# Expert tiles of 816 rows instead of 832, with the last partial tile transposed first

## The chip, the cores and the metric

The kernel runs on one core of a Trainium2 chip. The core has five engines with an instruction stream each: TensorE (PE in the profile; PEld is its weight load), VectorE (DVE), ScalarE (ACT), GpSimd (POOL) and SyncE (SP), which here only issues transfers. The metric is the device time of one execution, from the first to the last instruction with what lies around them, in microseconds (us). The median over several runs is compared.

## The reference

```python
# attention: delta rule, state (48 x 48) per batch and head, 768 steps
for t in range(S):
    y[:, :, t] = q[:, :, t] @ state
    v_old = state.T @ k_n[:, :, t]
    state = state + beta[t] * outer(k_n[:, :, t], v[:, :, t] - v_old)
x = y.transpose(0, 2, 1, 3).reshape(3072, 384)
# router: top 2 of 8 experts for each token
noisy = x @ w_gate + log1p(exp(x @ w_noise)) * noise
top2, top2_w = two largest of noisy, their softmax
# experts
for e in range(8):
    for k in range(2):
        mask = top2[:, k] == e
        h = maximum(x[mask] @ w1[e], 0)          # 384 -> 1024
        out[mask] += top2_w[mask, k] * (h @ w2[e])   # 1024 -> 384
```

All values are float32. There are 3072 tokens with two experts each, so an expert has 768 tokens on average. Evaluated with its own seed, the reference sends 711, 771, 789, 774, 756, 744, 807 and 792 tokens to the experts 0 to 7.

## The kernel before, in words

**Two stages.** `deltanet` (L470) computes attention and the router up to about 390 us; its order comes from a planner (`Jobs`, with costs and due times). While it runs, tokens are entered in a list for each expert (`tokens_x` in HBM: token number, gate, place of its row in `rows_y`), and the first five tiles of expert 0 are computed. The change touches nothing that the planner orders.

**How an expert is laid out.** Each expert takes a fixed number of rows, `ROWS = TILES * 128 + MORE`: six full tiles of 128 tokens and one partial tile of `MORE` tokens. An index past the list is out of bounds and is skipped by the transfers. `count` is the largest number of tokens of any expert; if it is over `ROWS`, a last branch (L1855) computes the remaining tiles of all experts one by one.

**What one expert does.** The loop `for e in range(1, E)` (L1775) is a written-out order, and every engine runs its own instructions in that order. For each expert:

- `first` (L1632) multiplies by `w1` as a fast block product: 20 products of blocks (`FACTORS`), each for two 128-column pieces, in place of 24. One operand is a block of `w1` or a sum of blocks (`s_w`), the other is half of the expert's rows (`RH = ROWS // 2` columns of `xe`, or a sum `s_x`). `PLAN` is the list of products, copies, additions and ReLUs, with the PSUM bank (`inner`) of each. The float32 products are two PE instructions each in the trace, so an expert has 80 of them (L1591, tile `inner`), then ACT copies (L1658) or DVE adds (L1652) the result to `hT`.
- `sums_of_hidden` (DVE, L1579) forms sums of the hidden blocks, and `second` (L1660) multiplies by `w2` in blocks of 192 columns (L1591, 192 columns moved), with the gate applied by DVE (L1487, L1491). It treats six full tiles as three pairs (tile i of the first three with tile i of the last three). The three are `pairs[0]`, `pairs[1]` and `pairs[2]`.
- `last_rows` (L1694) does the partial tile: its `MORE` tokens are the stationary operand, and two results are built side by side, one in partitions from 0, one in partitions from 64 (`halves`); DVE adds both (L1706).
- `put` (L1782) issues POOL's indirect transfer that adds a tile to the output (L460).

**The next expert's rows.** During expert e, POOL gathers the rows of expert e+1 into `xr` (`load_rows`, L405), SP rearranges them to `xq` with 16 transfers (`regroup`, L1605), and DVE turns 32 x 32 blocks (`turns`, L1615) into `xe`. The turns are a generator of seven instructions: six for full tiles (three chunks k of the first three tiles, then three of the last three) and one for the partial tile. They are placed two at a time behind the steps n = 5, 6, 3, 7, 4 of `second` for `pairs[0:2]` (L1826). After the turns that follow n = 7, DVE runs five additions of `SUMS_X` on the new `xe` (L1832), then the gates of n = 4; the first of them reads the bank `outer[0]`, which step n = 1 of `pairs[2]` overwrites (L1837).

The columns of `hT` and `xe` are laid out as first three tiles, partial tile, last three tiles: `full = [0:MAIN], [MAIN+MORE:ROWS]` with `MAIN = 384`, while `half` cuts at `RH`.

**Expert 0's remainder** is `rest` (L1709): tile 5 and the partial tile, `cols = 128 + MORE` columns, 48 PE instructions at L1742, then L1752 for tile 5 and L1757 for the partial tile, which is built side by side as in `last_rows`.

Of the kernel before, what the change touches and what calls it, by code (L numbers as in the profile page):

```python
# [21 lines left out]
Q = 32  # L22
QS = 128 // Q
TILES = 6
MORE = 64
EARLY_BANK = 2, (0, 1, 2)
EARLY = {2: [(0, 2)], 4: [(2, 4), (4, 5)]}
EARLY_TILES = 5
# [4 lines left out]
PUT_IN_RULE = -1  # L33
ROWS = TILES * 128 + MORE
META = 3
# [202 lines left out]
def kernel(  # L238
# [51 lines left out]
    KT = DM // 128  # L290
    FT = F // 128
    NT = N // 128
# [110 lines left out]
    def take_rows(got, index, units):  # L403

        d = nc.gpsimd.indirect_dma_start(  # L405
            out=got, out_offset=None, in_=rows_y[0 : units * 128],
            in_offset=bass.IndirectOffsetOnAxis(ap=index, axis=0),
            bounds_check=units * 128 - 1, oob_is_err=False,
        ).ins
        tc.add_to_no_dep_group("taken", d)  # L410
        for n, i in stored:
            if n < units:
                tc.add_manual_dep(d, i.name, SYNC, reason="rows stored before they are read")
        return d

    metas_x = const.tile([128, E, TILES + 1, META], FP32, name="metas_x")
    early_x = [const.tile([128, DM], FP32, name=f"early_x{i}") for i in range(EARLY_TILES)]
    early_meta = const.tile([128, EARLY_TILES, META], FP32, name="early_meta")
    rest_x = const.tile([128, TILES + 1 - EARLY_TILES, DM], FP32, name="rest_x")
    rows_in = [128] * TILES + [MORE]  # L420

# [15 lines left out]
    def place_of(meta):  # L437
        return meta[..., 2:3].bitcast(I32)
# [1060 lines left out]
    with ExitStack() as ectx:  # L1499
# [18 lines left out]
        FT2, MAIN = FT // 2, TILES // 2 * 128  # L1518
# [5 lines left out]
        xr = moe.tile([128, TILES + 1, DM], FP32, name="xr")  # L1524
        xq = moe.tile([128, QS, TILES + 1, DM // QS], FP32, name="xq")
        xe = moe.tile([128, KT, ROWS], FP32, name="xe")
# [11 lines left out]
        half = [slice(0, RH), slice(RH, ROWS)]  # L1538
        full = [slice(0, MAIN), slice(MAIN + MORE, ROWS)]

# [54 lines left out]

        def load_rows(e):
            for i, size in enumerate(rows_in):
                take_rows(xr[0:size, i], place_of(metas_x[0:size, e, i]), NT)

        def regroup(queues=(nc.sync,)):  # L1600

            for g in range(QS):
                tiles = TILES + (g * Q < MORE)
                for c in range(QS):
# [7 lines left out]
        def turns():  # L1612

            def turn(out, in_):
                return lambda: nc.vector.transpose(out=out, in_=in_)  # L1615

            some = TILES // 2
            for i in range(2):
                for k in range(KT):
                    yield turn(  # L1620
                        xe[:, k, full[i]].rearrange("p (i g x) -> p i g x", i=some, g=QS),
                        xq[:, :, i * some : (i + 1) * some, k : DM // QS : KT].rearrange(
                            "p g i j -> p i g j"
                        ),
                    )
            more = MORE // Q
            yield turn(
                xe[:, :, MAIN : MAIN + MORE].rearrange("p k (g x) -> p k g x", g=more),
                xq[:, 0:more, TILES].rearrange("p g (j k) -> p k g j", k=KT),
            )  # L1630

        def first(a1, sums):  # L1632

# [75 lines left out]
        def rest():  # L1709
# [6 lines left out]
            load_metas(1)  # L1716
            load_metas(0)
            load_rows(1)
            for i, size in enumerate(rows_in[t0:]):
                take_rows(rest_x[0:size, i], place_of(metas_x[0:size, 0, t0 + i]), NT)  # L1720
# [26 lines left out]
            for turn in turns():  # L1747
                turn()
# [26 lines left out]
        for e in range(1, E):  # L1775
# [36 lines left out]
            if follows:  # L1812
                load_rows(e + 1)
                regroup()
                add_up(nc.gpsimd, SUMS_W, blocks[0])
# [5 lines left out]
            for emit in of_hidden[1][2:4]:  # L1821
                emit()
            both(2, 1)
            turning = turns() if follows else iter(())
            sums_x = SUMS_X if follows else []
            for n in (5, 6, 3, 7, 4):  # L1826
# [28 lines left out]
    with tc.If(count > ROWS):  # L1855
        for e in range(E):
            with tc.tile_pool(name=f"left{e}", bufs=1) as pool:
                w1e, w2e = load_weights(weight_tiles(pool), e)
                earlier, added = added, []
                for i in range(TILES, NT):  # L1860
# [8 lines left out]
                    xr = pool.tile([128, DM], FP32, name="xrl")  # L1869
                    take_rows(xr, place_of(meta), NT)  # L1870
                    got = pool.tile([128, DM], FP32, name="gotl")
                    xe = pool.tile([128, KT, 128], FP32, name="xel")
# [53 lines left out]
```

## Time and profile before

| | |
|---|---|
| median of 4 runs | 834.45 us (827.36 to 837.58) |
| profiled execution | 833.76 us |
| its span, first to last instruction | 831.9 us |
| mean granted TensorE clock | 0.868 over the span, 1.00 in the experts |
| PE busy, whole span | 736.6 us (89%) |
| DVE, POOL, ACT busy | 542.2, 419.0, 308.6 us |
| one expert of the loop, start to start | 58.5 us |

The experts 1 to 7 run from 409.05 to 818.2 us; in front of them is `rest` from 391 us, behind them some 13.6 us in which the last rows are added to the output. A busy PE row contains overlap between matmuls, so what one matmul costs is read from the distance between starts, not from its mean duration.

### The profile page before, as it was taken

The page shows a single profiled execution, that of the slowest core. Times are in us where ns is not written, and L with a number is a line of the kernel's source. Part 1 is how long each engine was busy: PE and PEld are TensorE (multiplying, and loading weights), DVE is VectorE, ACT ScalarE, POOL GpSimd, SP SyncE. Part 2 cuts the span into 40 slices and gives each one's busy share as a digit, 9 for nine tenths or more (in the row PEclk, how much of TensorE's full clock was granted, in tenths as well). Part 3 has the DMA queues.
Part 4 walks back from the last instruction along what each step waited for, and adds up shares of the span by engine and source line. Part 5 has one row for each costly group of instructions (what it writes and reads, how often), then busy time and mean ns, then how long its engine had stood idle before and what let it go on. Part 6 is the DMA issues. An engine that isn't in the chain of part 4 may idle for free.

```text
span 831.9 us, 22382 instructions
## 1 busy us (share of the span) xinstructions
PE 736.6 (89%) x9319; PEld 578.4 (70%) x9319; DVE 542.2 (65%) x1100; ACT 308.6 (37%) x728; POOL 419.0 (50%) x408
## 2 busy tenths in 40 slices
PE   4656888888888874999999999999999999999993
PEld 3545777777767764877659668678578587596593
DVE  7999959898663150301578588488587686785841
ACT  3757486766452521321250250340430520511500
POOL 5030032011145324259678778787886886787032
PEclk9557867797665575999999999999999999999997
DMA  4457545322433110514835545545554446333031
GB/s 67 86 103 180 137 124 107 77 62 61 126 61 97 34 39 2 201 42 100 201 92 131 114 108 121 125 107 113 142 150 56 141 138 121 90 61 46 2 38 25
DMA packets 142719, 79.60 MB, mean 96 GB/s; under 512 B 118352, under 2 KB 139024, under 8 KB 141584
## 3 DMA queue, kind: packets, MB, share of 16 engines
q1 hardware_dynamic: 125840, 57.25, 26.6%
q0 software_dynamic: 12800, 19.80, 13.5%
q8 instruction: 75, 1.23, 0.6%
q10 hardware_dynamic: 3968, 1.03, 0.6%
q14 instruction: 36, 0.29, 0.1%
HBM read 49.85 MB, written 20.03 MB: 84 GB/s over the span
## 4 chain that ended last, share of the span: by engine, by line
PE 69%; issue 12%; DVE 10%; POOL 4%; ACT 2%; DMA 1%; SPq 0%; POOLq 0%; DVEq 0%
PE inner L1591 24%; PE outer L1591 11%; PE pair L630 5%; PE pair L1343 3%; PE pair L1367 3%; PE single L1022 3%; PE pair L1007 2%; PE single L614 2%; DVE w2e L761 2%; PE pair L970 2%; POOL out_dram L460 2%; PE pair L903 2%; PE pair L948 2%; PE single L839 2%; PE inner L1702 2%
## 5 line engine op out<-in xcount | busy, mean ns | idle before, releaser
L1658 ACT ACTIVATE hT<-inner 128x416 f32<-128x416 f32 x112 | 57.8, 517 | 261.0 <-PE inner L1591 255.6
L1652 DVE TENSOR_TENSOR hT<-hT,inner 128x416 f32<-128x416 f32 x182 | 105.5, 587 | 63.5 <-PE inner L1591 55.5
L460 POOL DMA_INDIRECT out_dram<-sums,metas_x x51 | 83.4, 1635 | 93.0 <-DVE sums L1491 67.3
L441 POOL DMA_INDIRECT tokens_x<-meta,slot x48 | 48.5, 1010 | 64.6 <-issue 19.9
L1591 PE MATMUL inner<-s_x,w1e 128*128 128x416 f32 x196 | 78.7, 512 | 0.0
L912 POOL TENSOR_TENSOR v<-v,norms 128x384 f32<-128x384 f32 x24 | 24.1, 1019 | 101.0 <-DVE norms L744 49.1
L405 POOL DMA_INDIRECT xr<-rows_y,metas_x x49 | 55.8, 1138 | 19.4 <-issue 13.0
L1647 ACT ACTIVATE hT<-hT 128x416 f32<-128x416 f32 x112 | 59.9, 547 | 12.1 <-DVE hT L1652 6.5
L1591 PEld LDWEIGHTS inner<-s_x,w1e 128*128 128x128 f32 x196 | 37.2, 190 | 31.2 <-issue 28.8
L1591 PE MATMUL inner<-xe,w1e 128*128 128x416 f32 x140 | 58.1, 513 | 0.0
L1591 PE MATMUL outer<-t_w,hT 128*128 128x192 f32 x336 | 58.0, 326 | 0.0
L1591 PE MATMUL inner<-s_x,s_w 128*128 128x416 f32 x140 | 56.9, 512 | 0.0
L1591 PEld LDWEIGHTS outer<-t_w,hT 128*128 128x128 f32 x336 | 55.2, 190 | 0.0
L1557 POOL TENSOR_TENSOR w1e<-w1e 128x256 f32<-128x256 f32 x63 | 52.7, 845 | 2.4
L1591 PE MATMUL outer<-w2e,hT 128*128 128x192 f32 x280 | 50.7, 328 | 0.3
L1591 PEld LDWEIGHTS outer<-w2e,hT 128*128 128x128 f32 x280 | 46.1, 190 | 4.3 <-issue 2.1
L1591 PEld LDWEIGHTS inner<-s_x,s_w 128*128 128x128 f32 x140 | 26.6, 190 | 22.3 <-issue 22.3
L819 ACT COPY w<-tt_tb 32x256 f32<-32x256 f32 x96 | 38.6, 402 | 6.9 <-DVE tt_tb L796 5.2
L1591 PEld LDWEIGHTS inner<-xe,w1e 128*128 128x128 f32 x140 | 26.4, 190 | 20.7 <-issue 16.8
L1591 PE MATMUL outer<-t_w,s_h 128*128 128x192 f32 x224 | 40.6, 329 | 0.0
L1487 DVE TENSOR_SCALAR sums<-outer,metas_x 128x192 f32<-128x192 f32 x70 | 27.8, 412 | 18.4 <-PE outer L1591 17.7
L1591 PEld LDWEIGHTS outer<-t_w,s_h 128*128 128x128 f32 x224 | 36.6, 190 | 4.2 <-issue 4.2
(202 smaller groups left out, 1625.3 us busy)
## 6 DMA issues: line engine op xcount, KB each, us to landing
w1e<-in_moe_w_dram SPq DMA_DIRECT2D x8, 1536.0 KB
w2e<-in_moe_w_dram SPq DMA_DIRECT2D x8, 1536.0 KB
v<-in_v_dram SPq DMA_DIRECT2D x48, 96.0 KB
qp<-in_q_dram SPq DMA_DIRECT2D x48, 96.0 KB
out_dram<-empty SPq DMA_DIRECT2D x4, 1152.0 KB
rows_y<-y SPq DMA_DIRECT2D x24, 192.0 KB
xq<-xr SPq DMA_DIRECT2D x52, 84.0 KB
kp<-in_k_dram SPq DMA_DIRECT2D x88, 48.0 KB
```

The source lines that it names most:

```text
L405: d = nc.gpsimd.indirect_dma_start(out=got, out_offset=None, in_=rows_y[0 : units * 128], in_offset=bass.IndirectOffsetOnAxis(ap=index, ax ...
L441: d = nc.gpsimd.indirect_dma_start(out=tokens_x, out_offset=bass.IndirectOffsetOnAxis(ap=slot, axis=0), in_=meta, in_offset=None, bounds_c ...
L460: d = nc.gpsimd.indirect_dma_start(out=out, out_offset=bass.IndirectOffsetOnAxis(ap=index, axis=0), in_=got, in_offset=None, bounds_check= ...
L630: nc.tensor.matmul(out[to(z, b), z, j], kT[rows_of[z], j, crossed(z, b)], rhs(z, j, b), start=(j == 0), stop=(j == NP - 1), skip_group_che ...
L819: lambda rows=rows, cols=cols, w64=w64, tt=tt: nc.scalar.copy(w64[rows, :, cols], tt[rows]),
L1022: nc.tensor.matmul(p_l, xTs(n)[:, do], router["wgn"][:, do], start=(do == 0), stop=(do == KT - 1),)
L1487: nc.vector.tensor_scalar_mul(got, p, gate)
L1557: engine.tensor_tensor(out=block(to), in0=block(x), in1=block(y), op=ALU.add if sign == "+" else ALU.subtract,)
L1591: nc.tensor.matmul(p, lhsT, rhs, start=opens and i == 0, stop=i == len(products) - 1, skip_group_check=True,)
L1647: nc.scalar.activation(h, h, ACTF.Relu)
L1652: nc.vector.tensor_tensor(out=h, in0=h, in1=p, op=ALU.add if sign > 0 else ALU.subtract)
L1658: nc.scalar.mul(h, p, float(sign))
```

## The change

An expert takes 816 rows: `MORE` is 48, so the partial tile has 48 tokens, `RH` is 408 and `cols` in `rest` is 176. The gather of the partial tile and its turn still handle 64 rows (`TAKEN`), since the turn works on blocks of 32. The 16 extra columns that this turn writes (432 to 447 of `xe`) belong to the last three tiles, so the partial turn is yielded first and the full turns overwrite them. Places, number and sizes of the full turns, the gathers and the 16 transfers to `xq` are the same; the transfers that add to the output (`put`, `rows_in`) take 48 rows of the partial tile. `PLAN`, `FACTORS` and the order of the steps in `second` are as they were.

```diff
-MORE = 64
+MORE, TAKEN = 48, 64
@@ load_rows
             for i, size in enumerate(rows_in):
-                take_rows(xr[0:size, i], place_of(metas_x[0:size, e, i]), NT)
+                n = TAKEN if i == TILES else size
+                take_rows(xr[0:n, i], place_of(metas_x[0:n, e, i]), NT)
@@ turns
-            some = TILES // 2
+            some, more = TILES // 2, TAKEN // Q
+            yield turn(
+                xe[:, :, MAIN : MAIN + TAKEN].rearrange("p k (g x) -> p k g x", g=more),
+                xq[:, 0:more, TILES].rearrange("p g (j k) -> p k g j", k=KT),
+            )
             for i in range(2):
                 for k in range(KT):
                     yield turn(
...
-            more = MORE // Q
-            yield turn(
-                xe[:, :, MAIN : MAIN + MORE].rearrange("p k (g x) -> p k g x", g=more),
-                xq[:, 0:more, TILES].rearrange("p g (j k) -> p k g j", k=KT),
-            )
```

## Prediction

> **What bounds the kernel now.** I read the page's busy table and slices first, to see in what state the changed stage is: the experts, from 391 us on, the last 21 of the 40 slices.
>
> ```profile
> PE 736.6 (89%) x9319; PEld 578.4 (70%) x9319; DVE 542.2 (65%) x1100; ACT 308.6 (37%) x728; POOL 419.0 (50%) x408
> ...
> PE   4656888888888874999999999999999999999993
> ...
> PEclk9557867797665575999999999999999999999997
> ```
>
> PE shows 9 in all of them but the last, at the full granted clock. The busy time by stretch says the same (stretch and length, then PE, PEld, DVE, ACT, POOL, clock, DMA share, GB/s), for one whole expert and for the first product of another:
>
> ```profile
> 526.20:584.70 58.50, 58.46 (x265) 43.53 (x265) 42.98 (x76) 16.38 (x32) 45.22 (x40) 1.00 0.48 119
> ...
> 467.70:495.70 28.00, 28.00 (x83) 15.27 (x82) 18.62 (x31) 15.37 (x31) 22.80 (x19) 1.00 0.49 134
> ```
>
> PE is busy for the whole expert; POOL is free for 23% of it, DVE for 27%, ACT for more. But a busy row can hide a short stall, so I read the chain of waits (start, length, what) next:
>
> ```profile
> 401.16 5.16 PE outer L1752 x16
> 406.32 2.73 PE outer L1757 x16
> ...
> 584.67 27.93 PE inner L1591 x80
> ...
> 620.40 2.60 PE outer L1591 x16
> ```
>
> The 80 matmuls of the first product are 27.93 / 80 = 0.349 us apart with 416 columns; those of 192 columns are 2.60 / 16 = 0.1625 us apart. So a column costs (0.349 - 0.1625) / 224 = 0.83 ns, and nothing but PE sets that pace. The chain leaves PE at one place of every expert that prepares another one. The timelines of DVE and of PE show it in expert 4:
>
> ```profile
> 628.24 0.42 DVE L1491 SCALAR_TENSOR_TENSOR sums<-outer,metas_x,sums 128x192 f32<-128x192 f32 x1 [0.67 <-PE outer L1591]
> 628.58 0.43 DVE L1615 STREAM_TRANSPOSE xe<-xq 128x192 f32<-128x192 f32 x1
> 629.04 1.60 DVE L1557 TENSOR_TENSOR s_x<-xe 128x416 f32<-128x416 f32 x3
> 630.67 0.59 DVE L1557 TENSOR_TENSOR xe<-xe 128x416 f32<-128x416 f32 x1
> 631.18 0.58 DVE L1557 TENSOR_TENSOR s_x<-xe,s_x 128x416 f32<-128x416 f32 x1
> 631.68 0.74 DVE L1487 TENSOR_SCALAR sums<-outer,metas_x 128x192 f32<-128x192 f32 x2
> ```
>
> ```profile
> 630.64 1.46 PE L1591 MATMUL outer<-t_w,s_h 128*128 128x192 f32 x8
> 632.15 1.57 PE L1591 MATMUL outer<-w2e,hT 128*128 128x192 f32 x8
> ```
>
> PE could go on at 630.64 + 8 x 0.1625 = 631.94 us, but the bank is free only when the first L1487 is through (631.68 + 0.42). It starts at 632.15: 0.21 us late, and the second matmul then comes 0.27 us after the first in place of 0.16. In front of that gate stand the partial turn and five additions. Six experts pay this; expert 7 turns nothing and does not.
>
> **The change, part by part.** *Shorter first product.* 416 columns become 408: 8 x 0.833 = 6.66 ns for each of 80 matmuls, 0.533 us an expert, 3.73 us for seven. All of it is on the path if DVE and ACT keep up. I set PLAN's list against the trace of expert 4 and took, for every reuse of a bank, the time from the end of the copy or add that frees it to the start of the next matmul into it. The least is 0.97 us. Between such a pair of events lie a few matmuls, so the squeeze is some tens of ns, and the adds shrink too. Nothing waits.
>
> *Expert 0's remainder.* 48 matmuls (L1742) go from 192 to 176 columns: 48 x 16 x 0.833 ns = 0.64 us. From 393.0 to 406.2 us PE is busy 13.11 of 13.20, ACT 2.69, so it counts in full.
>
> *The other products.* `second` moves 192 columns as before, `sums_of_hidden` and the gates work on full tiles: nothing.
>
> *The partial tile's product* has 48 stationary columns in place of 64, and no row of the trace has 48. With 64 (L1757) 16 matmuls take 2.73 us, with 128 (L1752) and the same 384 moving columns 5.16 us: the two halves of 64 run side by side. So the block costs between 2.73 us and, if halves of 48 took turns, 5.16 us. A gain is excluded, since a pair lasts as long as its 384 moving columns, which stay. I take 2.73, the nearer row: 48 from the same start partitions 0 and 64.
>
> The page "TensorEngine Tiling (Array Packing)" of the Trainium skill (Tiling Modes; Tile-to-Partition Mapping, Restrictions) knows column tiles of 32 and 64 only, and asks that the active columns not exceed the tile's. By it 48 sits in a tile of 64 and costs what 64 does, and only 32 would gain; no row here shows 48.
>
> *Turns.* There are still seven, of the same sizes, but the partial one leads, so the slot after n = 7 now holds a full turn. The timeline has 0.46 us from the start of the partial turn to that of the first addition (628.58 to 629.04), and 0.60 us for a full turn (two from 625.98 to the next DVE instruction at 627.17). That is 0.14 us more in front of the late gate. The five additions start 0.51 us apart for 416 elements, so 8 fewer give at most 10 ns each, 0.05 us together. The anchor, DVE's gate at 628.24, is paced by PE and its 192-column steps do not change, so PE's stall grows by 0.09 to 0.16 us (0.16 if the additions gain nothing and the full turn takes the 0.62 us of one led in by a gate). I take 0.12: 6 x 0.12 = 0.72 us of loss.
>
> *The transfers to `xq`* do not shorten, while DVE reaches its turns 0.53 us earlier. The tightest expert is 2 (SP's issues, then DVE's first turn):
>
> ```profile
> 498.93 3.16 SPq L1605 DMA_DIRECT2D xq<-xr  x3
> ...
> 503.95 1.30 DVE L1615 STREAM_TRANSPOSE xe<-xq 128x384 f32<-128x384 f32 x2
> ```
>
> There the last issue ends at 502.09 and the last packet of these transfers at 503.25, by the packets' own times; the turn begins 0.70 us later, after 0.03 us of idle DVE, so I take 0.70 us as the least distance. In the experts 3, 4 and 5 it is 1.0, 1.3 and 1.6 us, so expert 3 too has less to spare than 0.53. But the partial turn needs only the first 8 of the 16 transfers and is done first: it covers 0.46 of the 0.53 us. What is left is 0.07 us in expert 2, behind which DVE still idles before n = 7. I cost it at nothing; without that cover each late expert could lose up to its 0.53 us.
>
> *Gathers, additions to the output.* The gather is the same. POOL's addition of the partial tile takes 48 rows where 64 took 1.44 us and 128 take 1.56: POOL has 13 us free in an expert, nothing. The weight loads are issued at PE's own pace, one expert ahead.
>
> **Sum.** -3.73 - 0.64 + 0.72 = -3.65 us. The profiled execution took 833.76 us (span 831.9), so 830.1; on the median, 834.45 - 3.65 = **830.8 us**, 0.44% faster. That is less than this kernel can show: four runs lay between 827.36 and 837.58, and about 1% is what a measurement tells from no change.
>
> The page "TensorE: Matmul & The Clock Gate" (Back-to-back issue gap) gives a warm gap of N / 2.4 + 2.5 ns, one clock a column. By it 8 columns would be 3.3 ns and 560 matmuls an estimated 1.9 us, half of my term. The rows above have two clocks a column (0.83 ns at 2.4 GHz) in float32, so the measurement decides; the constant of 2.5 ns agrees with 0.349 us less 416 x 0.833 ns.
>
> **The rivals.**
>
> *Slower: halves of 48 take turns.* Each of eight partial blocks (seven of L1702, one of L1757) goes from 2.73 to 5.16 us, 2.43 x 8 = 19.4 us, so 834.45 - 3.65 + 19.4 = **850.2 us**. It decides from 0.46 us a block (3.65 / 8), where the gain is gone. For it: only 64 is seen to overlap. Against it: partitions 0 to 47 and 64 to 111 are apart as before. Chance 0.13.
>
> *The gain of the product is waited for.* If turns or transfers hold PE in the experts 1 to 6, their period stays 58.5 us, and only expert 7 and the remainder gain, 0.53 + 0.64: **833.3 us**. For it: expert 2's start without slack, and that gathers and transfers are paced by POOL and SP. Against it: 1 us and more in later experts, and the partial turn as cover. Chance 0.10.
>
> *The stall goes.* If DVE came earlier to the gate than I think, the 0.21 + 0.10 us of stall vanish in six experts, and 0.72 are not lost: -3.73 - 0.64 - 1.86 = -6.2 us, **828.2 us**. Against it: the queue in front of the gate gets longer. Chance 0.07.
>
> *It doesn't do what it says:* an expert over 816 tokens would open the last branch. A tile there has 48 first products (5.36 us for such a group, L1343) and 16 second ones (5.16 us), and there are 8 x 18 tiles: 1.5 ms more. The reference's largest expert has 807 tokens, so below 0.01.
>
> **How the numbers follow.** The forecast has 0.67, the rivals 0.13, 0.10 and 0.07, and 0.03 is for what I don't see, such as halves that start 1632 bytes into a row instead of 1664. Around 830.8 the median of a few runs can lie 4 to 5 us off, and the second and third rival fall into that: the range is 826 to 838 us. The slow rival is left out of it. Faster by over 1% (below 826.1) needs the forecast or the vanished stall with luck: 0.12. Slower by over 1% (above 842.8) is the slow rival and some of the unseen: 0.17. Within 1%: 0.71.
>
> **What would show it.** In the profile after, the 80 matmuls of an expert should take 27.4 us, the experts start 58.05 us apart, the partial block stay at 2.73 us, and the late gate be preceded by a full turn, with PE 0.3 to 0.4 us late after it. A block of 5.16 us shows the slow rival; a period of 58.5 us with DVE idle ahead of a full turn shows the waiting one. The prediction is wrong above all if 48 columns do not overlap.

## The result, and the profile after

The changed kernel took 828.93 us (median of 52 runs, 822.38 to 834.86) against 833.19 us for the kernel before (78 runs, 826.55 to 841.21). The ratio is 0.9953, with a 95% interval from 0.9939 to 0.9967: 0.47% faster, where 0.44% was forecast, and inside 1% as forecast.

The profiled execution has a span of 830.7 us, only 1.2 us under the 831.9 before. That difference is no measure of the change: in the profile after, attention ended later. The first matmul of expert 0's remainder starts at 394.50 us, before the change at 391.58, and the change touches nothing ahead of it. From there to PE's last matmul it is 422.57 us after and 426.67 us before, 4.10 us less. All experiments below are read by this stretch and by the distance between neighbouring experts (first matmul of the 80 to first matmul of the next 80), since these repeat to a few hundredths of a us: 427.33 and 427.31 us in two profiles of one kernel. One profile, of 832 rows with three turns first, is an exception, told there. What follows PE's last matmul, the last additions to the output, is not in the stretch: it took 13.6 us before and after, and up to 14.6 us in the other profiles.

The page after, busy table and slices, as shown of before:

```profile
PE 725.7 (87%) x9319; PEld 570.4 (69%) x9319; DVE 539.6 (65%) x1100; ACT 306.8 (37%) x728; POOL 416.8 (50%) x408
...
PE   4656889888867773999999999999999999999993
```

The stage is still full of PE. One expert by stretch (length, then busy PE, PEld, DVE, ACT, POOL, clock, DMA share, GB/s):

```profile
527.46:585.46 58.00, 57.88 (x265) 43.39 (x265) 42.77 (x76) 16.17 (x32) 44.78 (x40) 1.00 0.49 120
```

58.00 us in place of 58.47, again at the full granted clock; PE now has 0.12 us of visible idle time, where it had 0.04. The chain of waits after, for expert 4:

```profile
585.46 27.40 PE inner L1591 x80
...
620.66 2.60 PE outer L1591 x16
...
628.49 0.42 DVE sums L1491
628.91 0.61 DVE xe L1616
629.52 1.47 DVE s_x L1557 x3
...
632.09 0.34 DVE sums L1487
632.43 0.04 issue
632.47 1.57 PE outer L1591 x8
634.04 2.72 PE inner L1702 x16
```

The 80 matmuls take 27.40 us (27.93 before), 16 matmuls of `second` take 2.60 us as before, and the partial block with 48 stationary columns takes 2.72 us (2.73 with 64). The turn in front of the late gate is now a full one. The timelines of DVE and PE at the same place, after:

```profile
628.49 0.42 DVE L1491 SCALAR_TENSOR_TENSOR sums<-outer,metas_x,sums 128x192 f32<-128x192 f32 x1 [0.69 <-PE outer L1591]
628.83 0.70 DVE L1616 STREAM_TRANSPOSE xe<-xq 128x384 f32<-128x384 f32 x1
629.44 1.54 DVE L1557 TENSOR_TENSOR s_x<-xe 128x408 f32<-128x408 f32 x3
631.01 0.58 DVE L1557 TENSOR_TENSOR xe<-xe 128x408 f32<-128x408 f32 x1
631.51 0.57 DVE L1557 TENSOR_TENSOR s_x<-xe,s_x 128x408 f32<-128x408 f32 x1
632.01 0.73 DVE L1487 TENSOR_SCALAR sums<-outer,metas_x 128x192 f32<-128x192 f32 x2
```

```profile
630.89 1.46 PE L1591 MATMUL outer<-t_w,s_h 128*128 128x192 f32 x8
632.47 1.57 PE L1591 MATMUL outer<-w2e,hT 128*128 128x192 f32 x8
```

PE could go on at 630.89 + 8 x 0.1625 = 632.19 and starts at 632.47, 0.28 us late, where it was 0.21. So the expert gained 0.53 us in the first product and 0.01 in the partial block, and lost about 0.07 us at the gate, which together is the 0.47 us.

### The profile page after: what moved, and what is told of

Read it like the earlier page. It is cut to its first block, busy times and chain, and to the rows that moved or that the text cites. A ratio compares the mean times of both kernels' runs of the same rounds, so it can differ in the third digit from the quotient of the medians.

```text
span 830.7 us, 22410 instructions
## 1 busy us (share of the span) xinstructions
PE 725.7 (87%) x9319; PEld 570.4 (69%) x9319; DVE 539.6 (65%) x1100; ACT 306.8 (37%) x728; POOL 416.8 (50%) x408
## 4 chain that ended last, share of the span: by engine, by line
PE 67%; DVE 13%; issue 12%; ACT 2%; SPq 2%; POOL 2%; DMA 1%; POOLq 0%; DVEq 0%; ACTq 0%
PE inner L1591 25%; PE outer L1591 13%; PE pair L630 4%; PE pair L1343 3%; DVE w2e L761 3%; PE pair L1367 3%; PE pair L903 2%; PE pair L1007 2%; PE single L614 2%; PE inner L1702 2%; DVE w2e L765 2%; PE pair L948 2%; PE pair L970 2%; PE single L1022 2%; DVE w1e L765 2%
## 5 line engine op out<-in xcount | busy, mean ns | idle before, releaser
L1658 ACT ACTIVATE hT<-inner 128x408 f32<-128x408 f32 x112 | 57.1, 511 | 259.5 <-PE inner L1591 256.9
L1652 DVE TENSOR_TENSOR hT<-hT,inner 128x408 f32<-128x408 f32 x182 | 104.1, 578 | 61.3 <-PE inner L1591 53.0
L1591 PE MATMUL inner<-s_x,w1e 128*128 128x408 f32 x196 | 77.5, 506 | 0.0
L405 POOL DMA_INDIRECT xr<-rows_y,metas_x x49 | 54.4, 1111 | 20.0 <-issue 13.6
L1647 ACT ACTIVATE hT<-hT 128x408 f32<-128x408 f32 x112 | 59.1, 540 | 11.7 <-DVE hT L1652 6.4
L1591 PE MATMUL inner<-xe,w1e 128*128 128x408 f32 x140 | 57.2, 507 | 0.0
L1591 PE MATMUL inner<-s_x,s_w 128*128 128x408 f32 x140 | 56.0, 506 | 0.0
```

What stands on the lines that cost most here:

```text
L405: d = nc.gpsimd.indirect_dma_start(out=got, out_offset=None, in_=rows_y[0 : units * 128], in_offset=bass.IndirectOffsetOnAxis(ap=index, ax ...
L1591: nc.tensor.matmul(p, lhsT, rhs, start=opens and i == 0, stop=i == len(products) - 1, skip_group_check=True,)
L1647: nc.scalar.activation(h, h, ACTF.Relu)
L1652: nc.vector.tensor_tensor(out=h, in0=h, in1=p, op=ALU.add if sign > 0 else ALU.subtract)
L1658: nc.scalar.mul(h, p, float(sign))
```

## The experiments

All are against the kernel before. The lengths come from one profile each; the last column is the ratio of times with its 95% interval. Of the order alone, which was run twice, the row shows the second run.

| kernel | one expert (2 to 6) | remainder to PE's last matmul | ratio |
|---|---|---|---|
| before | 58.47 us | 426.67 us | 1 |
| changed | 58.00 | 422.57 | 0.9953 (0.9939 to 0.9967) |
| order alone | 58.58 | 427.31 | 0.9991 (0.9966 to 1.0015) |
| partial turn fourth | 58.00 | 422.55 | 0.9938 (0.9906 to 0.9970) |
| halves one after the other | 60.57 | 443.17 | 1.0194 (1.0136 to 1.0252) |
| three turns first | 57.62 | 420.27 | 0.9916 (0.9882 to 0.9949) |
| 808 rows | 57.70 | 420.13 | 0.9931 (0.9892 to 0.9970) |
| 808 rows, three turns first | 57.34 | 417.99 | 0.9896 (0.9859 to 0.9934) |
| 832 rows, three turns first | 58.16 | 426.48 | 0.9968 (0.9929 to 1.0006) |
| gates first | 58.72 | 426.89 | 0.9997 (0.9968 to 1.0027) |

**The order of the turns alone.** Half of the change: the partial turn leads, but rows stay 832.

```diff
 # kernel before
-            some = TILES // 2
+            some, more = TILES // 2, MORE // Q
+            yield turn(xe[:, :, MAIN : MAIN + MORE]..., xq[:, 0:more, TILES]...)
             for i in range(2):
...
-            more = MORE // Q
-            yield turn(xe[:, :, MAIN : MAIN + MORE]..., xq[:, 0:more, TILES]...)
```

> 832 rows, the partial turn first: the second half of the change alone. Theory (shorter products bring the gain, the turn order costs): the 80 matmuls stay at 27.93 us, PE is 0.28 to 0.37 us late behind n = 4 in place of 0.21, an expert that prepares another takes 58.55 to 58.65 us, and the time is 0.4 to 1 us over the kernel before, a ratio of 1.0005 to 1.0012. Rival (the turn order, or chance, brings the gain): a ratio near 0.995 with 832 rows too.

The expert took 58.58 us, in the range of the theory, but the time came out at 832.01 us, a ratio of 0.997 (0.9939 to 1.0001), lower than the theory's 1.0005 to 1.0012; the interval holds the rival's 0.995. The profile was of an execution in which attention ended only at 397 us, so the kernel was run once more:

> The same kernel as in the first run of the order alone (832 rows, partial turn first), since that one's profile is of an execution with a long attention stage and its ratio of 0.997 reached from 0.994 to 1.000, below what the theory gave. Theory: 58.58 us an expert again, PE 0.31 to 0.33 us late at n = 1, and a ratio whose interval holds 1.001. Rival (the order of the turns brings part of the gain): the ratio stays near 0.997 and the stretch from the remainder of expert 0 to PE's last matmul is under the 426.7 us of the kernel before.

This run was on another chip, where both kernels were faster, 803.56 us against 804.10, and the ratio is 0.9991 (0.9966 to 1.0015): its interval holds the theory's 1.001 and excludes the 0.995 of the first rival. It does not exclude the second rival's 0.997; that one falls by its other sign, the stretch. The profile repeats the first one: 58.58 us an expert, PE 0.31 us late at the gate on average, 427.31 us for the stretch (427.33 in the first run), 0.64 us more than before and not less. Why the first ratio came out lower was not found. The chain, with a full turn in front of five additions of 416 columns:

```profile
597.99 0.42 DVE sums L1491
598.40 0.60 DVE xe L1615
599.00 1.49 DVE s_x L1557 x3
...
601.61 0.34 DVE sums L1487
601.95 0.04 issue
601.99 1.57 PE outer L1591 x8
```

So the order brings none of the gain; it costs 0.11 us in each of six experts.

**The partial turn fourth.** The order undone as far as the overlap of the columns allows it: three full turns, the partial one, three full turns.

```diff
 # changed kernel
-            yield turn(xe[:, :, MAIN : MAIN + TAKEN]..., xq[:, 0:more, TILES]...)
             for i in range(2):
+                if i == 1:
+                    yield turn(xe[:, :, MAIN : MAIN + TAKEN]..., xq[:, 0:more, TILES]...)
                 for k in range(KT):
```

> 816 rows, the partial turn behind the three full turns of the first half instead of ahead of them; the last slot still holds a full turn. Theory: as the changed kernel, 58.0 us an expert, a ratio of 0.995, with DVE idle for up to 0.5 us ahead of the first turn in experts 2 to 4, which PE does not feel. Rival (the transfers to xq hold the turns, and the partial turn in front is what covers them): experts 2 to 4 take 58.3 to 58.5 us and the ratio is 0.997 or more.

58.00 us an expert and 422.55 us for the stretch, the same as the changed kernel. One expert by stretch, and the first turns of another on DVE, which has no idle time ahead of them:

```profile
522.25:580.25 58.00, 57.89 (x266) 43.40 (x265) 42.73 (x76) 16.18 (x32) 44.84 (x40) 1.00 0.49 120
```

```profile
615.86 1.30 DVE L1616 STREAM_TRANSPOSE xe<-xq 128x384 f32<-128x384 f32 x2
```

DVE was idle ahead of the first turn in expert 1 only, for 0.24 us, and not in the experts 2 to 4, where up to 0.5 us were expected. The waiting rival falls: without the partial turn in front, the transfers to `xq` hold nothing that PE feels.

**The halves one after the other.** What the slow rival said 48 columns would do. The partial tile's product is summed in one place by the same 16 matmuls, and one gate takes it; `rest` likewise.

```diff
 # changed kernel, last_rows
-                    p[halves[fo % 2]], hT[:, fo, MAIN : MAIN + MORE], w2e[:, fo],
-                    start=(fo < 2), stop=(fo >= FT - 2), skip_group_check=True,
+                    p[0:MORE], hT[:, fo, MAIN : MAIN + MORE], w2e[:, fo],
+                    start=(fo == 0), stop=(fo == FT - 1), skip_group_check=True,
```

> 816 rows, the partial tile's product summed in one place, partitions 0 to 47, not side by side: what the slow rival said 48 columns would do. Theory (PE sets the time, nothing else would wait there): each of eight blocks goes from 2.72 to 5.16 us, 19.5 us more than the changed kernel, about 848.5 us or a ratio of 1.018. Rival (another engine has the expert's period, and PE's gain is only partly visible): under 12 us more, a ratio below 1.010.

849.19 us (the run of the kernel before beside it: 834.27), a ratio of 1.0194, and 20.60 us more in the stretch than the changed kernel. The chain:

```profile
577.62 5.29 PE inner L1701 x16
582.91 6.70 PE outer L1591 x40
589.61 27.40 PE inner L1591 x80
```

A block costs 5.29 us (5.16 expected), 2.57 more than side by side, and 8 x 2.57 = 20.6: all of it shows. This prices the rival that was given 0.13, and it shows that what is added to PE here is added to the kernel.

**Three turns in the first slot.** If the late gate is DVE's queue of a turn and five additions, moving the turn out of it ends the delay.

```diff
 # changed kernel
-                for turn in (next(turning, None), next(turning, None)):
+                for turn in [next(turning, None) for _ in range(3 if n == 5 else 2)]:
```

> 816 rows, three turns behind n = 5 in place of two, so that none is left behind n = 7. Theory (the late gate is DVE's queue of one turn and five additions): 0.6 us leave that queue, PE's 0.28 us of delay and the 0.10 us of refill vanish in six experts, an expert takes 57.6 to 57.7 us, 1.7 to 2.3 us less than the changed kernel, a ratio of 0.9925 to 0.9935. Rival (the bank is late for another reason, or the longer first slot makes PE late elsewhere): 58.0 us an expert, a ratio of 0.995.

57.62 us an expert, 2.30 us less in the stretch than the changed kernel, a ratio of 0.9916 (0.9882 to 0.9949). DVE does three turns where the changed kernel did two (the timeline of the changed kernel, that of this one, then the chain):

```profile
621.07 1.10 DVE L1616 STREAM_TRANSPOSE xe<-xq 128x192 f32<-128x192 f32 x2
```

```profile
615.28 1.71 DVE L1616 STREAM_TRANSPOSE xe<-xq 128x192 f32<-128x192 f32 x3
```

```profile
620.07 7.80 PE outer L1591 x48
627.87 2.72 PE inner L1702 x16
630.59 6.70 PE outer L1591 x40
637.29 7.88 PE inner L1591 x23
```

The chain no longer leaves PE: 48 matmuls without a break where a gap stood behind the 40th. An expert gained 0.38 us, 0.28 of delay and 0.10 of slow restart.

**The gates first.** The other way to free the gate: the additions move behind it.

```diff
 # changed kernel
-                if n == 7:
+                if n == 4:
                     add_up(nc.vector, sums_x[0:5], xb)
```

> The changed kernel with the five additions behind the gates of n = 4 instead of in front of them. Theory (DVE is busy without a break from n = 7 to the end of the additions, so the queue moves on): PE is on time at n = 1 of the last pair, but DVE then comes late to the gates behind it and PE loses 0.3 to 0.9 us at a later step; an expert takes 57.9 to 58.5 us. Rival (only the one gate is late, the order of DVE's work around it is enough): 57.6 us an expert as with the turns moved.

58.72 us an expert, slower than the kernel before and outside the range I gave. The mechanism is the theory's, its size was not: PE is on time at n = 1 of the last pair but loses 1.00 us at n = 7 of that pair, where I had 0.3 to 0.9. The PE timeline, and DVE's gate in front of the late step:

```profile
635.33 1.47 PE L1591 MATMUL outer<-w2e,s_h 128*128 128x192 f32 x8
637.64 1.57 PE L1591 MATMUL outer<-t_w,hT 128*128 128x192 f32 x8 [0.84 <-DVE sums L1487]
```

```profile
637.17 0.42 DVE L1487 TENSOR_SCALAR sums<-outer,metas_x 128x192 f32<-128x192 f32 x1
```

The eight matmuls from 635.33 should be followed at 636.64. DVE, which now has the five additions (2.6 us) between the gates of n = 4 and this one, reaches the gate that frees the bank only at 637.17. So DVE has no slack between n = 7 and the end of the additions; a turn could be moved ahead of that stretch, but the additions could not be pushed further into it.

**808 rows.** The same step once more by half its size, which also moves the start of a half from 1632 to 1616 bytes.

```diff
 # changed kernel
-MORE, TAKEN = 48, 64
+MORE, TAKEN = 40, 64
```

> 808 rows (40 in the partial tile), all else as in the changed kernel. Theory (each column of the first product costs 0.83 ns in 80 matmuls of seven experts): the 80 matmuls take 27.13 us in place of 27.40, an expert 57.7 to 57.75 us, the remainder of expert 0 0.3 us less; 2.2 us less than the changed kernel, a ratio of 0.992 to 0.993. Rival (where a half starts in its row matters: 1616 bytes here, 1632 in the changed kernel, 1664 before): the matmuls or DVE's additions do not shorten by the same step as from 832 to 816.

57.70 us an expert, 2.44 us less in the stretch than the changed kernel (2.2 expected; PE's delay at the gate also fell, from 0.28 to 0.25 us), a ratio of 0.9931 (0.9892 to 0.9970). The chain has

```profile
577.31 27.13 PE inner L1591 x80
```

So 416, 408 and 404 columns give 27.93, 27.40 and 27.13 us: 0.066 to 0.068 us a column, which is 80 x 0.83 to 0.85 ns. The start of a half in its row, 1664, 1632 or 1616 bytes, makes no difference to PE.

**808 rows and three turns first.**

> 808 rows and three turns in the first slot. Theory: both gains add, 57.35 us an expert, 4.2 to 4.5 us less than the changed kernel, a ratio of 0.989 to 0.991. Rival (with the late gate gone and the products shorter, another wait appears: the rows' transfers, or DVE in the first slot): an expert over 57.5 us.

Both gains add: 57.34 us an expert, 4.58 us less than the changed kernel, a little over the range. The ratio is 0.9896 (0.9859 to 0.9934), 822.11 us against 830.28 for the kernel before beside it. It is the fastest of the kernels here. By stretch, for one expert:

```profile
458.11:515.45 57.34, 57.34 (x266) 43.37 (x265) 42.70 (x76) 16.06 (x32) 44.85 (x40) 1.00 0.50 121
```

PE is busy from end to end. The largest expert has 807 tokens, so 808 is as low as these inputs allow without the last branch.

**832 rows and three turns first.**

> The kernel before with three turns in the first slot (the partial one still last, now in the third slot with one full turn). Theory (the late gate was there before the change, 0.21 us and 0.10 us of refill): an expert takes 58.15 to 58.2 us in place of 58.47, 1.9 us less, a ratio of 0.9975 to 0.998. Rival (the late gate only matters with a full turn in the last slot): no change in the expert's period.

58.16 us an expert, 0.31 less than the kernel before, as expected: the late gate was there before the change. The ratio's interval, 0.9929 to 1.0006 around 0.9968, holds the forecast, but also no change at all, so the period decides. The stretch is only 0.19 us shorter, because in this execution the remainder of expert 0 was 1.68 us longer than before (19.08 in place of 17.40). The chain and the stretch show where, and the kernel before over the same length stands last:

```profile
386.86 6.82 PE inner L1742 x30
```

```profile
386.80:390.40 3.60, 3.54 (x12) 3.55 (x13) 2.96 (x6) 0.33 (x2) 3.14 (x4) 0.54 0.81 23
```

```profile
393.00:396.60 3.60, 3.51 (x21) 3.51 (x22) 2.99 (x6) 0.98 (x4) 3.14 (x4) 1.00 0.77 20
```

The granted clock was 0.54 for 3.6 us at the start of the remainder, and 12 matmuls ran where the kernel before had 21 in the same 3.6 us at 1.00. The 30 matmuls took 6.82 us in place of 5.14, which is the 1.68 us. Why the clock was lower there was not tried.

## Why the prediction was right, point by point

**The time: right, in part by luck.** The median of 828.93 us lies 1.9 us under the forecast 830.8. Of these, 1.3 us come from the kernel before, whose median over 78 runs is 833.19 and not the 834.45 of the first four. As a bare time it is nearer to the 828.2 of the vanished stall than to the forecast, and the range of 826 to 838 us also held this rival and the waiting one. The ratio tells them apart: the forecast is 830.8 / 834.45 = 0.9956, the waiting rival 0.9986, the vanished stall 0.9925, the slow rival 1.019, and the interval from 0.9939 to 0.9967 holds the forecast alone. Of the signs named for the profile, one was missed: PE is 0.28 us late at the gate, not 0.3 to 0.4. The others came within 0.05 us.

**The first product: right.** 0.533 us an expert was forecast, 27.93 to 27.40 is 0.53. That DVE and ACT keep up holds too: no new wait appears in those 27.4 us, and 404 columns shorten them by the same step.

**Expert 0's remainder: right, a little small.** 0.64 us forecast, 17.40 to 16.69 = 0.71 us measured from its first matmul to the first expert's. The 0.64 counted only the 48 matmuls; the transposes and copies of 48 rows ahead of them were left out.

**The partial block: right.** 2.73 us taken, 2.72 measured, and the price of the other end was shown to be real: 5.29 us where the halves do not overlap. The page "TensorEngine Tiling (Array Packing)" of the Trainium skill (Restrictions) asks of the number of columns only that it not exceed the tile's; 48 columns at 2.72 us and 40 at 2.71 agree with that, neither gaining nor losing in a tile of 64. The 0.014 us between 64 and 48 lie in one distance, that from the block's second matmul to its third (0.367 to 0.353 us), and a weight load shortened by as much (137 to 123 ns).

**The turns: the right sign, the size too large.** 0.12 us an expert was forecast, with 0.09 to 0.16 as bounds; PE's delay grew from 0.21 to 0.28 us, by 0.07, which lies below the bounds. The order alone costs 0.11 us (58.47 to 58.58), less than the 0.14 that I read from the starts of a partial and a full turn. DVE's timeline of the order alone, with 416 columns as before, shows why:

```profile
634.44 0.70 DVE L1615 STREAM_TRANSPOSE xe<-xq 128x384 f32<-128x384 f32 x1
635.05 1.56 DVE L1557 TENSOR_TENSOR s_x<-xe 128x416 f32<-128x416 f32 x3
636.65 0.59 DVE L1557 TENSOR_TENSOR xe<-xe 128x416 f32<-128x416 f32 x1
```

The first addition starts 0.61 us after the start of the full turn (634.44 to 635.05), 0.15 us more than the 0.46 after that of the partial one. But the next instruction starts 1.60 us after the three additions (635.05 to 636.65), and behind the partial turn it was 1.63 us (629.04 to 630.67); the means over six experts are 1.59 and 1.63. So part of the longer turn comes back in the additions behind it, which a reading of the turn alone misses. The 408 columns of the changed kernel take another 0.03 us off the way from the turn to the gate (3.21 to 3.18 us on average), where up to 0.05 was forecast: 0.11 less 0.03 is the 0.07, but for rounding. Six experts lost about 0.3 to 0.4 us, not 0.72.

**The transfers to `xq`: right in the sum, wrong in one reading.** Nothing was forecast and nothing was lost. But I took 0.70 us as the least distance from the last packet to the first turn that needs it, and the partial turn's 0.46 us as the cover. In expert 4 after the change the last packet ends at 621.09 us by the packets' own times, and the second turn, the first full one, starts at 621.47, 0.38 us later, without idle time ahead of it. Where DVE was idle ahead of the turn, in expert 1 of the partial turn fourth, it was 0.52 us (441.63 to 442.15). And with no partial turn in front, the expert took 58.00 us all the same. The cover was not needed.

**The sum.** Forecast 3.65 us, measured 4.10 us in the stage of the changed kernel's profile. The terms: six experts at 0.475 us (2.85, forecast 2.48), the last expert 0.55 (0.53), the remainder 0.71 (0.64), which is 4.11. The excess of 0.45 us is the overpriced turn in six experts and the remainder. By the times of many runs the gain is 833.19 x (0.0033 to 0.0061) = 2.7 to 5.1 us, which holds both.

**The rivals.** The slow one would have cost 20.6 us and did not occur; the waiting one is excluded by the period of 58.00 us, which the partial turn fourth repeats without its cover; the stall did not vanish by itself, but could be removed by one line, for 2.30 us in the stretch, more than half of what the change brought.

## What to carry to other kernels

Where an engine is busy without a break, the price of a smaller operand is read from the distance between starts of two sizes of the same instruction, and it held here to a hundredth of a us per expert over three sizes. A chain of waits that leaves the bounding engine at one place only is worth reading instruction by instruction: here one line that moved a transpose to an earlier slot gave more than half as much as removing 2% of the rows. In this kernel work could be moved out of a queue into an earlier slot, but not into a later one, where the engine had no slack: the same gate freed by moving the additions back made the kernel slower by 0.25 us an expert than it was before the change.

## What the runs showed of the hardware that I had not expected

**The stage in front of the change varies most.** The remainder of expert 0, behind the same code, started at 391.58 us before, 394.50 after, 384.33 with 808 rows and three turns first, and at 361.00 in the second run of the order alone, which was on another chip. The experts took the same 58.58 us there as in the first run of that kernel. The granted clock in attention differs too. By stretch, the third hundred us of the kernel before, and of the order alone on the other chip (the clock is the third value from the end):

```profile
200.00:300.00 100.00, 84.91 (x2162) 73.04 (x2158) 50.48 (x140) 46.13 (x118) 33.32 (x36) 0.60 0.33 80
```

```profile
200.00:300.00 100.00, 79.43 (x2571) 70.71 (x2564) 55.98 (x162) 48.94 (x125) 41.52 (x44) 0.78 0.39 86
```

0.60 of the full clock and 2162 matmuls in one, 0.78 and 2571 in the other. Runs of the kernel before on one chip point the same way: the mean clock was 0.893 in the one of 823.66 us and 0.865 in the one of 835.53. What makes the clock differ was not tried, and whether the slower clock is the cause of the longer stage or goes along with it stays open. But for the one remainder above, the start of the remainder moves by many us from profile to profile and the experts do not, so a change of 0.5% in the experts took dozens of runs to show in the time, and one profile to show in the stage.

**A late matmul costs more than its delay.** Where PE waited 0.28 us for the gate, the second matmul then came 0.27 us after the first in place of 0.16. With the wait gone, both went: 0.38 us an expert in the changed kernel (58.00 to 57.62), and 0.31 us in the kernel before, where the delay was 0.21.
